# Converting the weights in units of 1024 columns, the low parts written over their own words

## The chip, the cores and the metric

The kernel runs on one core of a Trainium2 chip. The metric is the device time of one execution in microseconds (us). Before the change the median of three runs is 1238.58 us (1236.67 to 1239.37).

## The reference

An attention with random features comes first: 8 batches, 8 heads, 576 positions, 64 numbers each, 128 features. Its output, 4608 tokens of 512 numbers, goes through a gated layer.

```python
def phi(x):
    proj = np.einsum('bhsd,md->bhsm', x, omega)
    sq = np.sum(x * x, axis=-1, keepdims=True) / 2.0
    h = proj - sq
    h = h - np.max(h, axis=-1, keepdims=True)
    return np.exp(h) / np.sqrt(m)
...
kv = np.einsum('bhsm,bhsd->bhmd', k_p, v)
z = np.sum(k_p, axis=2)
num = np.einsum('bhsm,bhmd->bhsd', q_p, kv)
den = np.einsum('bhsm,bhm->bhs', q_p, z)[..., None] + 1e-06
...
gate = 1.0 / (1.0 + np.exp(-(x @ w_gate)))
val = x @ w_val
return (gate * val @ w_out).astype(np.float32)
```

The inputs of the attention are float32. The three weights, w_gate and w_val (512 x 1536) and w_out (1536 x 512), are float64. The kernel gets them as pairs of 32-bit words, a low and a high one, and turns them into float32 itself; this conversion is what is changed.

## The kernel before, in words

**Stages.** The program has four stages. In the first some 30 us only the attention of the first heads runs. Then, to about 510 us, the attention of all heads runs interleaved with a first pass of the gated layer: the tiles `gv` (L247), products of the tokens `xe` with the first 4 of 12 column tiles of the gate and value weights, `wh` and `wl`. From 600 us a second pass computes the other columns (`gw`, L351), and from about 965 us the output product follows (`po`, L465). The last two read weights that were converted during the attention and stored in DRAM as `w32`.

**Products in two parts.** A float32 matrix is split in a high part, rounded on ScalarE (ACT, L70), and a low part, the rest, subtracted on VectorE (DVE) or GpSimd (POOL) (L71); a product takes three matmuls. In the attention the inputs `rawk` and `rawq` are split into `hik`, `lok`, `hiq`, `loq`; `ppk` and `ppq` are their projections. DVE takes their maxima (`mxk`, `mxq`, L552), combines them with the norms (`hmk`, `hmq`, L556; `nb`, L574; `subq`, L613), forms `hq` (L615) for the queries, and ACT the exponentials `kpk` (L587) for the keys; `pkv`, `ptq`, `pnq`, `pxq` are the matmuls that follow, with `denq`, `invq`, `xq` on DVE (L643 to L649) between the last two.

**Conversion.** A unit is 1024 columns of weights. There are 18: the four units `e` (`first_weights`), whose result is split at once into `wh` and `wl` for the first pass, and 14 units `c` (`convert_weights`), to which four differences are added on POOL (L180) before they are stored as `w32` (L181). A unit lives in a tile `cv` of 7 x 512 words per partition, of which there are two in turn: 1024 results, 2048 words of raw pairs, and a scratch of 512. Two loads of 512 pairs each fill it (L144). Then `from_float64` runs for one half after the other: with the high word, five instructions on DVE make the float32 `t` of the high word (L78 clears the sign, L81 bounds it, L85 shifts it, L88 puts the sign back) and the power of two that belongs to it (L92, into the scratch `a`); L94 scales the low word by that power, in the scratch; and L96, on POOL, adds this to `t`. The second half's L78 writes the scratch that the first half's L96 reads.

**Order.** Python generators hand out the steps: one step of a conversion for every 32 steps of the attention (`EVERY`) at first, later one per step of the first pass. Each engine works through its own queue in order; the tile framework's scheduler places each instruction in that queue, as the lists below show, and inserts the waits on other engines. A DMA is issued by SP's queue, also in order.

Of the kernel before, what the change touches and what calls it, by code (L numbers as in the profile page):

```python
# [9 lines left out]
F32 = mybir.dt.float32  # L10
F32R = mybir.dt.float32r
AF = mybir.ActivationFunctionType
ALU = mybir.AluOpType
AX = mybir.AxisListType
U32 = mybir.dt.uint32
# [5 lines left out]
P = 128  # L21
# [10 lines left out]
LARGEST = float(np.uint32(0x47EFFE00).view(np.float32))  # L32
LEAST = float(np.uint32(0x38000000).view(np.float32))
# [8 lines left out]
WE = 2 * KC * P  # L42
WP = 512
# [24 lines left out]
def split(nc, hi, lo, x, lo_engine=None):  # L68

    nc.scalar.activation(out=hi, in_=x, func=AF.Copy)  # L70
    (lo_engine or nc.vector).tensor_tensor(out=lo, in0=x, in1=hi.bitcast(F32), op=ALU.subtract)  # L71


def from_float64(nc, t, a, bits):


    lo, hi = bits[:, :, 0], bits[:, :, 1]
    nc.vector.tensor_scalar(out=a, in0=hi, scalar1=0x7FFFFFFF, scalar2=None, op0=ALU.bitwise_and)  # L78

    f = a.bitcast(F32)  # L80
    nc.vector.tensor_scalar(  # L81
        out=f, in0=f, scalar1=LARGEST, scalar2=LEAST, op0=ALU.min, op1=ALU.max
    )

    nc.vector.tensor_scalar(  # L85
        out=t, in0=a, scalar1=3, scalar2=0x3FFFFFFF, op0=ALU.logical_shift_left, op1=ALU.bitwise_and
    )
    nc.vector.scalar_tensor_tensor(  # L88
        out=t, in0=hi, scalar=0xC0000000, in1=t, op0=ALU.bitwise_and, op1=ALU.bitwise_or
    )  # L90

    nc.vector.tensor_scalar(out=a, in0=t, scalar1=0xFF800000, scalar2=None, op0=ALU.bitwise_and)  # L92
    r = a.bitcast(F32)
    nc.vector.scalar_tensor_tensor(out=r, in0=lo, scalar=2.0**-52, in1=r, op0=ALU.mult, op1=ALU.mult)  # L94
    x = t.bitcast(F32)
    nc.gpsimd.tensor_tensor(out=x, in0=x, in1=r, op=ALU.add)  # L96


@with_exitstack
def attn_glu_kernel(ctx: ExitStack, tc, qT, kT, qn, kn, va, om, ident, w, out):  # L100
    nc = tc.nc
# [35 lines left out]

    def converted(cv, i):


        raw = [cv[:, (1 + h) * 2 * WP : (2 + h) * 2 * WP] for h in range(2)]
        for h in range(2):
            o = i + h * WP
            nc.sync.dma_start(out=raw[h].rearrange("p (n two) -> p n two", two=2), in_=w[:, o : o + WP, :])  # L144
        yield
        for h in range(2):
            from_float64(
                nc, cv[:, h * WP : (h + 1) * WP], cv[:, 6 * WP :],
                raw[h].rearrange("p (n two) -> p n two", two=2),
            )  # L150
            yield

    def first_weights(pool, tiles):

        for j in range(NE):
            cv = tiles(f"e{j}")
            ws[j] = wh, wl = [pool.tile([P, WE], F32R, name=f"{t}{j}") for t in ("wh", "wl")]
            steps = converted(cv, j * WE)
            next(steps)
            for i in range(2):  # L160
                next(steps)
                s = slice(i * WP, (i + 1) * WP)
                split(nc, wh[:, s], wl[:, s], cv[:, s].bitcast(F32), lo_engine=nc.gpsimd)
                yield

    def convert_weights(tiles, ns):

        for n in ns:
            cv = tiles(f"c{n}")
            for _ in converted(cv, NE * WE + n * 4 * Q):  # L170
                yield
            f = cv[:, : 4 * WP].bitcast(F32).rearrange("p (b q) -> p b q", q=Q)
            b, t = f[:, :4], f[:, 4:]
            for o, x, y in (
                (t[:, 0], b[:, 3], b[:, 0]),
                (t[:, 2], b[:, 2], b[:, 3]),
                (t[:, 1], b[:, 2], t[:, 0]),
                (t[:, 3], b[:, 1], t[:, 1]),
            ):
                nc.gpsimd.tensor_tensor(out=o, in0=x, in1=y, op=ALU.subtract)  # L180
            nc.sync.dma_start(out=w32[n], in_=f)  # L181
# [10 lines left out]
    def unit(pool, n, lo_engine=None):  # L192


        u = pool.tile([P, 2, N_OPS, Q], F32R, tag="u", bufs=UL if pool is late else UE, name=f"u{n}")
        units[n] = u[:, 0], u[:, 1]
        whole = u[:, 1].bitcast(F32)
        keep_order = pin if lo_engine else lambda x: x
        keep_order(nc.sync.dma_start(out=whole[:, :3], in_=w32[n, :, :3]))
        keep_order(nc.sync.dma_start(out=whole[:, 3:], in_=w32[n, :, 4:]))  # L200
        yield

        half = UL + UE <= n < UL + UE + EP
        for o, engine in ((slice(0, 3), nc.vector), (slice(3, N_OPS), lo_engine or nc.vector)):
            hi, lo, x = u[:, 0, o], u[:, 1, o], whole[:, o]
            if half:
                keep_order(nc.scalar.activation(out=hi, in_=x, func=AF.Copy, scale=0.5))
                keep_order(
                    nc.vector.scalar_tensor_tensor(
                        out=lo, in0=x, scalar=0.5, in1=hi.bitcast(F32), op0=ALU.mult, op1=ALU.subtract  # L210
                    )
                )
                continue
            keep_order(nc.scalar.activation(out=hi, in_=x, func=AF.Copy))
            keep_order(engine.tensor_tensor(out=lo, in0=x, in1=hi.bitcast(F32), op=ALU.subtract))
        yield
# [464 lines left out]
    def attention(pool):  # L681

        active = []
        while True:
            while True:
                kinds = [name[0][0] for name, _ in active]
                free = [
                    i for i, (name, needs, _) in enumerate(tasks[:AHEAD])
                    if (ready(Q) or name[1] == name[-1] == 0) and done.issuperset(needs) and kinds.count(name[0][0]) < ACTIVE[name[0][0]]
                ]  # L690
                if not free or len(active) >= AT_ONCE:
                    break
                name, _, make = tasks.pop(free[0])
                active.append((name, make(pool)))
            if not active:
                return
            name, steps = active.pop(0)
            if next(steps, steps) is steps:
                done.add(name)
            else:  # L700
                active.append((name, steps))
                yield

    def ready(n):

        return all(through[p] * P >= n for p in range(NP))
# [4 lines left out]
    with tc.tile_pool(name="early", bufs=1) as early:  # L711
        gates = first_pass()
        with tc.tile_pool(name="a", bufs=1, side="right") as pool:
            steps = attention(pool)

            def tiles(name):
                return pool.tile([P, 7 * WP], U32, tag="cv", bufs=2, name=name)

            conv = first_weights(early, tiles)
            cycle[:] = ["at", "at", "at", "gv"]  # L720
            n = 0
            while not ready(Q):
                next(steps, None)
                n += 1
                if n % EVERY == 0:
                    next(conv, None)
            cycle.clear()
            later = convert_weights(tiles, range(N_LATE))
            n = credit = 0
            while not ready(B * S):  # L730
                next(gates)
                credit += RATE if n >= 4 * NE - 2 else FIRST
                while credit >= 1 and not ready(B * S):
                    next(steps, None)
                    credit -= 1
                n += 1
                if next(conv, conv) is conv and n >= FROM:
                    next(later, None)
            for _ in later:
                pass  # L740
        late = ctx.enter_context(tc.tile_pool(name="late", bufs=1, side="right"))
        cycle[:] = ["at", "at", "at", "gv"]

        left = 2 * NE * (NCH + 1) - n
        started, parts = [], iter(())
        for n, _ in enumerate(gates):
            if n == 2:
                started = [unit(late, n) for n in range(UL)]
                for one in started:
                    next(one)  # L750
            elif started and n % 3 == 0:
                next(started.pop(0))
            if n == left - 2 * NE:
                parts = operands(0)
                x = next(parts)
            elif n > left - 2 * NE:
                next(parts, None)
        assert not started
# [107 lines left out]
```

## Time and profile before

| | |
|---|---|
| median of three runs | 1238.58 us |
| the profiled execution | 1239.43 us, of which its span is 1237.6 us |
| mean granted TensorE clock | 0.968 |
| ACT busy | 530.7 us (43%) |
| POOL busy | 542.7 us (44%) |
| share of the chain that ended last | PE 71%, DVE 12%, issue 7%, DMA 5%, POOL 3% |

PE is the matmul part of TensorE, PEld its weight load. The span runs from the first to the last instruction of the program; the execution's own time is 1.8 us longer. In a row of a group stand the line, the engine, the operation, the output and inputs by the program's names, the shapes, the count, then the busy time in us with the mean duration in ns, then the idle time of that engine just ahead of these instructions and what ended it. A line of a timeline has start and duration in us, then the same, with the idle time ahead of it and its releaser in square brackets.

### The profile page before, as it was taken

Reading aid. Unit: us, or ns where it says so; the run is one execution under the profiler, and the core shown is the slowest. Engines: PE = TensorE matmul, PEld = TensorE weight load, DVE = VectorE, ACT = ScalarE, POOL = GpSimd, SP = SyncE. Lnnn points to the kernel's source line nnn. Section 1 sums busy time; section 2 is a strip of 40 time slices with the busy share of each in tenths; the row PEclk is TensorE's granted clock in tenths of the full one; section 3 lists DMA queues with packets and bytes.
Section 4 is the critical chain, followed back from the end, with each engine's and each line's share of the span. In section 5 each row is a group of like instructions: output and inputs, shape, how many; then the busy total and the mean of one; then the engine's idle time right before and its main releaser. Section 6 shows DMA issues by size and latency. Waiting matters only on the chain.

```text
span 1237.6 us, 23990 instructions
## 1 busy us (share of the span) xinstructions
PE 1172.3 (95%) x8828; PEld 1109.8 (90%) x8828; DVE 864.5 (70%) x1907; ACT 530.7 (43%) x1164; POOL 542.7 (44%) x599
## 2 busy tenths in 40 slices
PE   6798989999898999899899999999998899999998
PEld 5788978798887888788899999999998899999998
DVE  4889888999698866433566656666569777777773
ACT  5556755565455463342423322232325344343331
POOL 2454365556457552131466666666666211111110
PEclk7798989999899999899899999999999999999999
DMA  7667767786657641461432333323337676666662
GB/s 247 213 199 228 210 219 253 238 268 237 226 182 252 223 153 39 139 202 52 152 128 106 123 135 124 121 93 125 124 135 267 203 226 195 188 191 189 198 191 94
DMA packets 104950, 219.43 MB, mean 177 GB/s; under 512 B 11136, under 2 KB 42112, under 8 KB 103040
## 3 DMA queue, kind: packets, MB, share of 16 engines
q1 hardware_dynamic: 87984, 198.94, 48.5%
q10 hardware_dynamic: 16848, 18.95, 4.4%
q8 instruction: 70, 1.15, 0.4%
q14 instruction: 48, 0.39, 0.1%
HBM read 141.82 MB, written 76.02 MB: 176 GB/s over the span
## 4 chain that ended last, share of the span: by engine, by line
PE 71%; DVE 12%; issue 7%; DMA 5%; POOL 3%; ACT 1%; SPq 1%; ACTq 0%; DVEq 0%; POOLq 0%
PE gw L351 27%; PE po L465 20%; PE gv L247 10%; PE pkv L595 4%; PE pnq L638 4%; PE ptq L626 2%; DVE mxq L552 2%; DVE hq L615 1%; DMA xr<-xT 1%; DMA xT<-xsq 1%; DMA rawk<-kT 1%; POOL loq L71 1%; DVE hmq L556 1%; PE ppk L547 1%; POOL xe L71 1%
## 5 line engine op out<-in xcount | busy, mean ns | idle before, releaser
L351 PE MATMUL gw<-xl,u 128*128 128x256 f32 x3024 | 364.6, 283 | 6.9 <-ACT p L362 3.6
L351 PEld LDWEIGHTS gw<-xl,u 128*128 128x128 f32 x3024 | 363.5, 191 | 7.9 <-DVE u L331 3.9
L465 PE MATMUL po<-u,yh 128*128 128x256 f32 x1512 | 272.4, 283 | 0.0
L465 PEld LDWEIGHTS po<-u,yh 128*128 128x128 f32 x1512 | 234.8, 191 | 0.0
L465 PE MATMUL po<-u,yl 128*128 128x256 f32 x756 | 214.0, 283 | 3.3 <-DVE yl L71 3.3
L247 PE MATMUL gv<-xe,wh 128*128 128x512 f32 (+1 forms) x640 | 201.0, 388 | 2.1 <-POOL xe L71 2.1
L70 ACT ACTIVATE yh<-yr 128x896 fp32r<-128x896 f32 x108 | 100.2, 950 | 156.8 <-PE po L465 86.3
L465 PEld LDWEIGHTS po<-u,yl 128*128 128x128 f32 x756 | 144.3, 191 | 3.9 <-DVE yl L71 3.9
L247 PEld LDWEIGHTS gv<-xe,wh 128*128 128x128 f32 x640 | 117.3, 194 | 20.1 <-POOL xe L71 4.5
L71 POOL TENSOR_TENSOR yl<-yr,yh 128x896 fp32r<-128x896 f32 x17 | 38.0, 2232 | 215.3 <-PE po L465 139.9
L247 PE MATMUL gv<-xe,wl 128*128 128x512 f32 (+1 forms) x320 | 125.8, 394 | 2.7 <-POOL wl L71 1.6
L71 DVE TENSOR_TENSOR yl<-yr,yh 128x896 fp32r<-128x896 f32 x91 | 103.0, 1144 | 31.5 <-PE po L465 19.1
L331 DVE TENSOR_TENSOR u<-gw,p 128x256 f32<-128x256 f32 x144 | 60.7, 422 | 59.2 <-PE gw L351 51.1
L595 PE MATMUL pkv<-v,kpk 128*128 128x66 f32 x512 | 84.4, 290 | 13.3 <-ACT kpk L587 12.6
L595 PEld LDWEIGHTS pkv<-v,kpk 128*128 128x128 f32 x512 | 77.0, 209 | 21.5 <-ACT kpk L587 19.8
L71 POOL TENSOR_TENSOR lok<-rawk,hik 128x256 fp32r<-128x256 f32 (+1 forms) x80 | 55.5, 712 | 68.0 <-ACT hik L70 67.6
L456 DVE TENSOR_TENSOR yr<-yr 128x128 f32<-128x128 f32 x144 | 60.1, 451 | 35.3 <-DMA yr<-ye 34.8
L71 POOL TENSOR_TENSOR xe<-xr,xe 128x512 fp32r<-128x512 f32 (+1 forms) x40 | 49.1, 1244 | 74.2 <-ACT xe L70 62.4
L71 POOL TENSOR_TENSOR loq<-rawq,hiq 128x256 fp32r<-128x256 f32 (+1 forms) x80 | 56.5, 718 | 55.5 <-ACT hiq L70 54.7
L587 ACT ACTIVATE kpk<-ppk,nb 128x128 f32<-128x128 f32 x256 | 69.8, 393 | 17.4 <-DVE nb L574 17.1
L638 PEld LDWEIGHTS pnq<-kv,qpq 128*128 128x128 f32 (+1 forms) x640 | 70.5, 189 | 6.5 <-ACT qpq L628 4.3
L638 PE MATMUL pnq<-kv,qpq 128*128 128x66 f32 (+1 forms) x640 | 74.9, 273 | 1.4 <-ACT qpq L628 1.2
(108 smaller groups left out, 2166.6 us busy)
## 6 DMA issues: line engine op xcount, KB each, us to landing
yl<-yl SPq DMA_DIRECT2D x36, 896.0 KB, 3.8
yr<-yl SPq DMA_DIRECT2D x72, 448.0 KB, 3.5
xr<-xT SPq DMA_DIRECT2D x68, 256.0 KB, 4.7
c<-w SPq DMA_DIRECT2D x28, 512.0 KB, 5.1
w<-c SPq DMA_DIRECT2D x14, 1024.0 KB, 4.5
v<-va SPq DMA_DIRECT2D x32, 330.0 KB, 3.4
natk<-kn SPq DMA_DIRECT2D x36, 256.0 KB, 4.2
natq<-qn SPq DMA_DIRECT2D x36, 256.0 KB, 3.9
```

The costliest lines, as they stand in the source:

```text
L70: nc.scalar.activation(out=hi, in_=x, func=AF.Copy)
L71: (lo_engine or nc.vector).tensor_tensor(out=lo, in0=x, in1=hi.bitcast(F32), op=ALU.subtract)
L247: nc.tensor.matmul(gv, lhsT=u[:, s], rhs=v, start=(m == 0), stop=(m == 3 * KC - 1))
L331: return nc.vector.tensor_tensor(out=o, in0=a, in1=b, op=ALU.add)
L351: nc.tensor.matmul(o, lhsT=u[:, k, s], rhs=v[:, kc, :], start=(first and m == 0), stop=(m == 5), skip_group_check=not first,)
L456: nc.vector.tensor_tensor(out=raw[:, o], in0=raw[:, a], in1=raw[:, b], op=op)
L465: nc.tensor.matmul(o, lhsT=u[:, i, :], rhs=v[:, k, :], start=(j + m == 0 and n in (1, 6, 5, 4)), stop=(j == NPAIR - 1 and m == 2), skip_gr ...
L552: nc.vector.tensor_reduce(out=m.rearrange("p t h -> p (t h)"), in_=pp, axis=AX.X, op=ALU.max)
L587: nc.scalar.activation(out=kp[t][:, h, :], in_=pp[:, 2 * i + h, :], func=AF.Exp, bias=nb[:, t - t0, h : h + 1], scale=SCALE,)
L595: nc.tensor.matmul(pkv[:, h, :], lhsT=kp[b * MID + i][:, h, :], rhs=v[:, i, h, :], start=(i == 0), stop=(i == MID),)
L626: nc.tensor.transpose(out=pt[:, i, :], in_=h_sb[:, i, :], identity=id_sb)
L638: nc.tensor.matmul(pn[r, 2 * i + h, :], lhsT=qp[:, 2 * i + h, r], rhs=kvs[u, p, bb][:, h, :], start=True, stop=True,)
```

## The change

`from_float64` now works on a whole unit, 1024 columns, in one go: six instructions on DVE and one on POOL per unit instead of twelve and two. There is no scratch: the first four steps run in place in the result tile, and the power of two (L93 in the new file) is written over the high words of the raw pairs, every second word, where L95 multiplies it with the low words in place; POOL's addition reads it from there. One load of 1024 pairs takes the place of two. The function is a generator that yields between the third and the fourth instruction, so that a unit still takes as many steps as before. The split of a unit `e` into `wh` and `wl` is done once for 1024 columns after the whole conversion, not after each half. The tile `cv` is 6 x 512 words.

```diff
-def from_float64(nc, t, a, bits):
+def from_float64(nc, t, bits):
     lo, hi = bits[:, :, 0], bits[:, :, 1]
-    nc.vector.tensor_scalar(out=a, in0=hi, scalar1=0x7FFFFFFF, scalar2=None, op0=ALU.bitwise_and)
-    f = a.bitcast(F32)
+    nc.vector.tensor_scalar(out=t, in0=hi, scalar1=0x7FFFFFFF, scalar2=None, op0=ALU.bitwise_and)
+    x = t.bitcast(F32)
     nc.vector.tensor_scalar(
-        out=f, in0=f, scalar1=LARGEST, scalar2=LEAST, op0=ALU.min, op1=ALU.max
+        out=x, in0=x, scalar1=LARGEST, scalar2=LEAST, op0=ALU.min, op1=ALU.max
     )
     nc.vector.tensor_scalar(
-        out=t, in0=a, scalar1=3, scalar2=0x3FFFFFFF, op0=ALU.logical_shift_left, op1=ALU.bitwise_and
+        out=t, in0=t, scalar1=3, scalar2=0x3FFFFFFF, op0=ALU.logical_shift_left, op1=ALU.bitwise_and
     )
+    yield
     nc.vector.scalar_tensor_tensor(
         out=t, in0=hi, scalar=0xC0000000, in1=t, op0=ALU.bitwise_and, op1=ALU.bitwise_or
     )
-    nc.vector.tensor_scalar(out=a, in0=t, scalar1=0xFF800000, scalar2=None, op0=ALU.bitwise_and)
-    r = a.bitcast(F32)
+    nc.vector.tensor_scalar(out=hi, in0=t, scalar1=0xFF800000, scalar2=None, op0=ALU.bitwise_and)
+    r = hi.bitcast(F32)
     nc.vector.scalar_tensor_tensor(out=r, in0=lo, scalar=2.0**-52, in1=r, op0=ALU.mult, op1=ALU.mult)
-    x = t.bitcast(F32)
     nc.gpsimd.tensor_tensor(out=x, in0=x, in1=r, op=ALU.add)
+    yield
...
     def converted(cv, i):
-        raw = [cv[:, (1 + h) * 2 * WP : (2 + h) * 2 * WP] for h in range(2)]
-        for h in range(2):
-            o = i + h * WP
-            nc.sync.dma_start(out=raw[h].rearrange("p (n two) -> p n two", two=2), in_=w[:, o : o + WP, :])
+        bits = cv[:, 2 * WP :].rearrange("p (n two) -> p n two", two=2)
+        nc.sync.dma_start(out=bits, in_=w[:, i : i + 2 * WP, :])
         yield
-        for h in range(2):
-            from_float64(
-                nc, cv[:, h * WP : (h + 1) * WP], cv[:, 6 * WP :],
-                raw[h].rearrange("p (n two) -> p n two", two=2),
-            )
-            yield
+        yield from from_float64(nc, cv[:, : 2 * WP], bits)
...
             next(steps)
-            for i in range(2):
-                next(steps)
-                s = slice(i * WP, (i + 1) * WP)
-                split(nc, wh[:, s], wl[:, s], cv[:, s].bitcast(F32), lo_engine=nc.gpsimd)
-                yield
+            next(steps)
+            yield
+            next(steps)
+            split(nc, wh, wl, cv[:, :WE].bitcast(F32), lo_engine=nc.gpsimd)
+            yield
...
-                return pool.tile([P, 7 * WP], U32, tag="cv", bufs=2, name=name)
+                return pool.tile([P, 6 * WP], U32, tag="cv", bufs=2, name=name)
```

The instructions also take other places in the queues. Three places follow. The new file is 7 lines shorter behind the conversion, so L587 of before is L580 there, L180 is L173, and so on.

On ACT, at about 33 to 40 us, before: `wh_289<-e_288` is the split of the first half of the first unit, `kpk_2_0` the first exponentials of the third head pair's keys.

```order
L70 ACTIVATE hiq_2_0_503<-rawq_2_0_477 128x256
L70 ACTIVATE hiq_3_0_513<-rawq_3_0_490 128x256
L70 ACTIVATE hiq_1_2_538<-rawq_1_0_265 128x256
L70 ACTIVATE wh_289<-e_288 128x512
L70 ACTIVATE hiq_0_2_557<-rawq_0_0_269 128x256
L501 ACTIVATE x2k_5_735<-natk_5_733 128x512
L587 ACTIVATE kpk_2_0_345<-ppk_2_0_318,nb_2_0_343 128x128 x4
```

The same place now:

```order
L70 ACTIVATE hiq_2_0_496<-rawq_2_0_470 128x256
L70 ACTIVATE hiq_3_0_506<-rawq_3_0_483 128x256
L70 ACTIVATE hiq_1_2_531<-rawq_1_0_265 128x256
L70 ACTIVATE hiq_0_2_550<-rawq_0_0_269 128x256
L580 ACTIVATE kpk_2_0_338<-ppk_2_0_311,nb_2_0_336 128x128 x4
L580 ACTIVATE kpk_2_2_343<-ppk_2_2_319,nb_2_0_336 128x128 x4
L580 ACTIVATE kmidk_2_4_348<-ppk_2_4_327,nb_2_0_336 128x128 x2
L580 ACTIVATE kpk_3_0_383<-ppk_3_0_356,nb_3_0_381 128x128 x4
L580 ACTIVATE kpk_3_2_388<-ppk_3_2_364,nb_3_0_381 128x128 x4
L580 ACTIVATE kmidk_3_4_393<-ppk_3_4_372,nb_3_0_381 128x128 x2
L593 ACTIVATE kv_2_0_411<-pkv_2_0_400 128x132
L70 ACTIVATE wh_289<-e_288 128x1024
```

The split stood four places ahead of the keys' exponentials; now it stands behind those of both head pairs and behind `kv_2_0`.

On POOL, at the first unit `c`, before (from about 133 us): L96 is the addition of a half, L180 the first of the four differences; the rows between are low parts for the attention.

```order
L96 TENSOR_TENSOR c_2882<-c_2882 128x512
L71 TENSOR_TENSOR lok_2_0_1873<-rawk_2_0_1810,hik_2_0_1872 128x256
L71 TENSOR_TENSOR lok_2_2_1877<-rawk_2_0_1810,hik_2_2_1876 128x256
L71 TENSOR_TENSOR lok_2_4_1881<-rawk_2_0_1810,hik_2_4_1880 128x128
L71 TENSOR_TENSOR loq_2_7_1920<-rawq_2_1_1268,hiq_2_7_1919 128x256
L71 TENSOR_TENSOR loq_3_7_1976<-rawq_3_1_1306,hiq_3_7_1975 128x256
L71 TENSOR_TENSOR lok_3_0_2064<-rawk_3_0_1990,hik_3_0_2063 128x256
L71 TENSOR_TENSOR lok_3_2_2068<-rawk_3_0_1990,hik_3_2_2067 128x256
L71 TENSOR_TENSOR lok_3_4_2072<-rawk_3_0_1990,hik_3_4_2071 128x128
L96 TENSOR_TENSOR c_2882<-c_2882 128x512
L180 TENSOR_TENSOR c_2882<-c_2882 128x256
```

The same unit now:

```order
L96 TENSOR_TENSOR c_2842<-c_2842 128x1024
L71 TENSOR_TENSOR lok_0_0_1479<-rawk_0_0_1233,hik_0_0_1478 128x256
L173 TENSOR_TENSOR c_2842<-c_2842 128x256 x4
L71 TENSOR_TENSOR lok_0_2_1483<-rawk_0_0_1233,hik_0_2_1482 128x256
L71 TENSOR_TENSOR lok_0_4_1487<-rawk_0_0_1233,hik_0_4_1486 128x128
```

One addition of 1024 stands where two of 512 stood nine places apart, and the unit comes earlier against the attention: ahead of `lok_0_0`, which before stood 15 places ahead of the unit's first addition.

On DVE, where the last unit `e` was converted, before (at about 104 to 108 us): L92 and L94 are that unit's second half; `denq` to `xq` are the divisions of two query tiles.

```order
L88 SCALAR_TENSOR_TENSOR e_1175<-e_1175 128x512
L503 TENSOR_REDUCE ssk_0_1263<-x2k_4_1456 128x8
L92 TENSOR_SCALAR e_1175<-e_1175 128x512
L643 TENSOR_SCALAR denq_1_4_1327<-pnq_1_4_1322 128x2
L94 SCALAR_TENSOR_TENSOR e_1175<-e_1175 128x512
L647 RECIPROCAL invq_1_4_1329<-denq_1_4_1327 128x2
L643 TENSOR_SCALAR denq_0_4_1342<-pnq_0_4_1337 128x2
L649 TENSOR_TENSOR xq_1_4_1331<-pnq_1_4_1322,invq_1_4_1329 128x128
```

The same divisions now:

```order
L608 SCALAR_TENSOR_TENSOR hq_0_4_1224<-ppq_0_4_1215,subq_0_4_1222 128x256
L496 TENSOR_REDUCE ssq_0_2101<-x2q_0_2104 128x8
L496 TENSOR_REDUCE ssq_0_2101<-x2q_1_2144 128x8
L636 TENSOR_SCALAR denq_1_4_1287<-pnq_1_4_1282 128x2
L78 TENSOR_SCALAR c_3132<-c_3132 128x1024
L640 RECIPROCAL invq_1_4_1289<-denq_1_4_1287 128x2
L636 TENSOR_SCALAR denq_0_4_1302<-pnq_0_4_1297 128x2
L642 TENSOR_TENSOR xq_1_4_1291<-pnq_1_4_1282,invq_1_4_1289 128x128
```

The unit `e` is done some 30 rows earlier there, and between `denq_1_4` and its reciprocal stands the first instruction of the second unit `c`, not the last of a unit `e`.

## The prediction

> **What bounds the kernel now.** I read the page's busy shares first, then the busy time by stage, then the conversion's own rows, then the chain of waits.
>
> ```profile
> PE 1172.3 (95%) x8828; PEld 1109.8 (90%) x8828; DVE 864.5 (70%) x1907; ACT 530.7 (43%) x1164; POOL 542.7 (44%) x599
> core 0: us, PE busy (x) PEld busy (x) DVE busy (x) ACT busy (x) POOL busy (x), PEclk, DMA share, GB/s
> 0.00:34.00 34.00, 21.86 (x106) 20.97 (x106) 15.90 (x34) 18.25 (x50) 10.20 (x20) 0.80 0.74 250
> 34.00:110.00 76.00, 63.38 (x441) 59.00 (x440) 64.31 (x159) 46.10 (x131) 38.92 (x42) 0.84 0.65 210
> 110.00:450.00 340.00, 320.02 (x2287) 286.80 (x2288) 292.53 (x745) 191.41 (x526) 183.16 (x215) 0.96 0.67 223
> 600.00:1237.00 637.00, 626.36 (x5217) 624.80 (x5216) 425.53 (x830) 215.88 (x336) 277.44 (x292) 1.00 0.47 155
> ```
>
> By the page the matmuls bound everything. The table by stage says where that is not all: from 600 us PE is busy 626 of 637 us at a clock of 1.00, and nothing of this change happens there. From 34 to 450 us PE is busy 383 of 416 us and runs at 0.84 and 0.96, while DVE is busy 357. Two engines near their limit hand work back and forth; a link on DVE shows as a gap on PE, and some gaps are followed by a lowered clock. Nearly all of the 18 conversions run there, the last addition of a `c` at 447.
>
> **The instructions themselves.** The rows of the tile `c` give minimum, median and maximum in ns; the three window rows are the busy time, up to 510 us, on DVE and POOL of tile `c`, on DVE, ACT and POOL of tile `e`, and on POOL of line 96.
>
> ```profile
> L78 DVE TENSOR_SCALAR c<-c x28: 409/424/1496, 102.4 to 434.1; 128x512 uint32<-128x512 uint32 x28
> L85 DVE TENSOR_SCALAR c<-c x28: 394/418/922, 114.8 to 440.5; 128x512 uint32<-128x512 uint32 x28
> L94 DVE SCALAR_TENSOR_TENSOR c<-c x28: 660/682/1350, 131.9 to 446.2; 128x512 f32<-128x512 uint32 x28
> L96 POOL TENSOR_TENSOR c<-c x28: 1269/1285/1662, 133.1 to 447.0; 128x512 f32<-128x512 f32 x28
> L180 POOL TENSOR_TENSOR c<-c x56: 722/740/1193, 154.3 to 450.5; 128x256 f32<-128x256 f32 x56
> 0.00:510.00 510.00, 99.64 (x168) 81.54 (x84) 0.94 0.62 207
> 0.00:510.00 510.00, 28.75 (x48) 5.29 (x8) 21.25 (x16) 0.94 0.62 207
> 0.00:510.00 510.00, 47.72 (x36) 0.94 0.62 207
> L615 DVE SCALAR_TENSOR_TENSOR hq<-ppq,subq 128x512 f32<-128x512 f32 x64 | 42.8, 679 | 0.1
> ```
>
> The last line is wanted for the slope and has its partner here:
>
> ```profile
> L615 DVE SCALAR_TENSOR_TENSOR hq<-ppq,subq 128x256 f32<-128x256 f32 x16 | 6.4, 412 | 0.0
> ```
>
> Per unit DVE now runs eight instructions with one input (0.42 us) and four with two (0.68): 6.1 us undisturbed, 18 x 6.1 = 109 of the 99.6 + 28.8 = 128.4 us that it is busy with them; the other 19 us are times when single ones took up to 1.5 us. For 1024 columns a two-input instruction goes from 0.412 over 0.679 by another 0.534 to 1.21 us. The one-input kind shows no second size: it lies between 0.42 (no growth) and 0.84 (double); I take 0.69, half of the other kind's slope, since 512 columns in 0.42 against 0.68 says that it moves them about twice as fast. A unit then costs 4 x 0.69 + 2 x 1.21 = 5.2 us, and 18 units save **16 us of DVE time** (36 down to 6 at the ends). POOL's addition grows by the slope from 0.740 to 1.285 to 2.37 us; 18 of them in place of 36 save 18 x (2.57 - 2.37) = **3.5 us of POOL time**.
>
> **Every second word.** L93 writes, L95 reads and writes, and POOL reads the high words at a step of two words. Reading so is in the trace: L78 reads the high words (0.424) where L85 reads a dense tile (0.418). Writing so is not, nor POOL reading so. From below I put nothing. From above: L93 takes 1.21 us instead of 0.69 (18 x 0.52 = 9 us of DVE), L95 and POOL's addition double (22 and 43 us). I take nothing, by L78, and keep the ends for the range.
>
> The Trainium skill's page "GPSIMD Engine Reference", section "Performance pitfalls for Q7 kernels", says that POOL pays half as much again per element when it reads with a step of more than 8 bytes. The step here is 8 bytes, so by the page it is free; were it over the limit, the 18 additions would take some 21 us longer, by the share below 4 us of the sum. No run here shows it yet.
>
> **What lies on the path.** In the chain that ended last, followed in order of time to 480 us, 52 pieces are DVE's conversion instructions, 7 are line 96, and 51 are the small DVE steps `hmq` and `subq`. First and last of each:
>
> ```profile
> 56.07 0.34 DVE e L78
> 440.54 0.34 DVE c L85
> 33.81 1.23 POOL e L96
> 415.51 1.24 POOL c L96
> 55.06 0.28 DVE hmq L556
> 469.45 0.68 DVE hmq L556 x2
> 0.00:510.00 510.00, 43.14 (x160) 0.94 0.62 207
> ```
>
> They sum to 30.8, 9.3 and 16.5 us; the window row is the busy time of `hmq` and `subq`. So 30.8 / 128.4 = 24% of the conversion's DVE time, 9.3 / 47.7 = 19% of POOL's additions and 16.5 / 43.1 = 38% of the small steps stand on the chain. Saved DVE time is worth 16 x 24% = **-3.9 us**, saved POOL time 3.5 x 19% = **-0.7**.
>
> **Waits removed.** The tile row names who held an instruction back (us, times):
>
> ```profile
>   POOL c L96: 6.9, 4
>   DMA c<-w: 2.6, 1
> L78 DVE TENSOR_SCALAR e<-e 128x512 uint32<-128x512 uint32 x8 | 4.5, 560 | 4.6 <-DMA e<-w 4.2 <-POOL e L96 0.5
> ```
>
> DVE stood 6.9 + 0.5 us at L78 until POOL had read the scratch. That goes: 7.4 x 24% = **-1.8**. What is late next is DVE's own queue, where 86% of the time from 34 to 450 us is work. The single load must land whole before L78 starts; of 36 halves two waited for a load (2.6 and 4.2 us), so its cover is the DVE work queued ahead. I put 0; if each of 18 units waited 2.6 us it would be 18 x 2.6 x 24% = +11. In SP's queue 18 issues fall away, which nobody waits for.
>
> **Longer holds.** This is what speaks against the change:
>
> ```profile
> 109.48 1.29 POOL L71 TENSOR_TENSOR wl<-e,wh 128x512 fp32r<-128x512 f32 x1 [0.74 <-ACT wh L70]
> 109.57 1.23 DVE L556 SCALAR_TENSOR_TENSOR hmq<-mxq,sqq 128x2 f32<-128x2 f32 x1
> ```
>
> An `hmq` of two columns took 1.23 us and ended 0.03 us after POOL's subtraction: small DVE steps with two inputs wait until POOL's instruction is over. One hold of 2.37 in place of two of 1.285 can cost 0 to 1.09 us more per unit, as DVE has work that is not held for less or more of it. I take a quarter, 0.27, since the medians above lie at the minima (most instructions are not held): 18 x 0.27 x 38% = **+1.9**; at the full 1.09, +7.5.
>
> The Trainium skill's "SBUF — State Buffer", section "Who interferes with whom", has the pair: a DVE instruction with two SBUF inputs contends with a POOL instruction that reads SBUF, and in DVE's two-port modes the loser waits for the whole instruction. The trace agrees (1.23 us here). Taken to the letter for every addition, the sum loses those 7.5 instead of 1.9.
>
> **Two gaps by name.**
>
> ```profile
> 35.06 0.63 ACT L70 ACTIVATE wh<-e 128x512 fp32r<-128x512 f32 x1 [1.22 <-POOL e L96]
> 36.82 1.36 PE L595 MATMUL pkv<-v,kpk 128*128 128x66 f32 x5 [2.80 <-ACT kpk L587]
> 106.25 1.15 DVE L94 SCALAR_TENSOR_TENSOR e<-e 128x512 f32<-128x512 uint32 x1
> 107.94 0.45 PE L655 MATMUL pxq<-id_sb,xq 128*128 128x128 f32 x1 [2.35 <-DVE invq L647]
> 110.83 0.58 PE L247 MATMUL gv<-xe,wl 128*128 128x256 f32 x1 [1.59 <-POOL wl L71]
> 105.00:114.00 9.00, 5.06 (x27) 4.51 (x25) 7.62 (x22) 3.82 (x10) 6.21 (x8) 0.62 0.59 157
> ```
>
> ACT stood 1.22 us ahead of `wh` with the keys' exponentials queued behind it, and PE waited 2.80 us for them; the order above puts `wh` behind them. At 110.83 PE waited 1.59 us for the last `wl`, which now comes earlier. Of the 4.4 us I book **-2.0**: 1.22 and half of 1.59, since 1.23 of POOL is in the share already.
>
> **The sum:** -3.9 - 0.7 - 1.8 + 1.9 - 2.0 = -6.5. A shortened link lets the next one end last, and PE, with 94% in 110 to 450 us, has little room; I keep 70%, -4.6. From the profiled execution's 1239.43 that is 1234.8; it stood 0.85 above the median of the runs, so **1234.0** in their terms.
>
> **Rivals.**
>
> Given back. PE's 94% decides, and the holds cost their full 7.5: -6.5 + 5.6 = -0.9, so 1237.7. For it: DVE's and POOL's queues are reordered everywhere, and the holds are seen. Against: half the additions, and the four L180 are untouched. 20%.
>
> Slower. A conversion instruction of 1.21 us, held by POOL for up to 2.37, stands ahead of one link of a division, as L94 stood ahead of `invq` at 106.25; PE then stops long enough to lose its clock. That place shows the price: a gap of 2.35, then 9 us at 0.62, which is 9 x 0.38 = 3.4 us; 5.8 together. One new place takes back the gain (-4.6 + 5.8 = +1.2), from the second on it is slower: +7.0, 1245.6. Against: there are 36 long two-input instructions now where there were 72 shorter ones. 20%.
>
> Better. The same price in the other direction: the places at 36 and 106 us keep their clock as well, -4.6 - 5.8 = -10.4, 1228.2. For it: the queue no longer has those rows ahead of the waiting ones. 15%.
>
> It doesn't do what it says. The step of two words costs L93 and L95 their upper ends: 31 us x 24% = +7.4 against -4.6, so 1241.4. Against: L78. 5%.
>
> **Numbers.** The forecast (1231 to 1236) has the other 40%. The range takes in the better case nearly whole, the slower one up to a single place with its holds: 1226 to 1244. Differences below 0.2% (2.5 us) count as none, about what a measurement of this kernel can tell. Faster: 40 + 15 = 55%. Same: 20% and a part of the others, 23%. Slower: 22%.
>
> **What would show it.** Two-input conversion rows at 1.21 us, one-input at 0.69 and line 96 at 2.37 with the minima near these; conversion on DVE at 105 to 115 us in place of 128; no wait of L78 on line 96; no PE gap by `kpk` at about 34 us; `hmq` and `subq` within 5 us of their 43. Fewer us at half clock before 510 us for the better case, more for the slower one. I am wrong if L93 or L95 lies above 1.3 us at its minimum, if L78 waits for loads in most units, or if the output product or the second pass changes by more than 2 us.

## The result, and the profile after

The forecast was 1234.0 us, faster. The changed kernel takes **1257.21 us** (median of 6 runs, 1250.85 to 1260.52) against 1237.62 before: a ratio of **1.0162, interval 1.0132 to 1.0191**, so slower by about 20 us. The profiled execution (1253.32 us, span 1251.5) is the second shortest of the six; it is 14 us longer than the profiled execution of before, where the medians differ by 20. One execution of the run with DVE's steps at the first halves' places, further down, was in a slower state of the chip and is left out of its median and ratio.

First the busy shares of the page after, then its busy time by stage; the columns are those of the prediction's table.

```profile
PE 1179.0 (94%) x8828; PEld 1115.9 (89%) x8828; DVE 857.7 (69%) x1799; ACT 531.4 (42%) x1160; POOL 543.9 (43%) x577
...
0.00:34.00 34.00, 21.57 (x106) 20.66 (x106) 15.90 (x35) 18.76 (x53) 11.14 (x21) 0.80 0.77 258
34.00:110.00 76.00, 66.47 (x367) 61.87 (x368) 58.03 (x117) 38.80 (x104) 33.26 (x29) 0.69 0.60 195
110.00:450.00 340.00, 307.65 (x2215) 275.18 (x2215) 283.79 (x644) 188.99 (x520) 186.88 (x199) 0.97 0.66 225
600.00:1237.00 637.00, 629.93 (x5228) 627.86 (x5227) 427.64 (x836) 222.99 (x347) 276.57 (x292) 0.99 0.48 161
```

From 34 to 110 us PE finished 367 matmuls where it had finished 441, at a clock of 0.69 where it had 0.84. Cut at 200 us, the same view of before and then of after says where the loss ends:

```profile
34.00:200.00 166.00, 147.44 (x1071) 138.18 (x1071) 142.02 (x364) 102.07 (x280) 81.66 (x93) 0.89 0.68 221
200.00:600.00 400.00, 376.66 (x2439) 325.84 (x2438) 281.04 (x682) 194.48 (x499) 173.40 (x195) 0.97 0.56 189
```

```profile
34.00:200.00 166.00, 140.50 (x920) 130.22 (x920) 132.68 (x292) 92.73 (x251) 78.69 (x79) 0.81 0.64 210
200.00:600.00 400.00, 377.36 (x2496) 327.81 (x2497) 278.84 (x632) 196.55 (x511) 177.49 (x187) 0.99 0.54 183
```

By 200 us 151 matmuls are missing. At 166 / 1071 = 0.155 us each, the mean before, that is an estimate of 23 us. From 200 to 600 us there are 57 more than before, which at 400 / 2439 = 0.164 us wins back 9. The 14 us that are left are the difference of the two profiled spans (1251.5 against 1237.6). PE idled 25.5 us in place of 18.6 from 34 to 200 us, and the lower clock (0.81 for 0.89 over 166 us) is up to 13 more.

The conversion's own rows, of the tile `c` after, and the busy time of the tiles `c` and `e` up to 510 us, of `hmq` (with `subq`) up to 530, where its last step lies now, and of line 96 up to 510, are as the prediction drew them:

```profile
L78 DVE TENSOR_SCALAR c<-c x14: 672/722/2376, 103.5 to 391.0; 128x1024 uint32<-128x1024 uint32 x14
L85 DVE TENSOR_SCALAR c<-c x14: 657/684/1674, 110.1 to 393.5; 128x1024 uint32<-128x1024 uint32 x14
L89 DVE SCALAR_TENSOR_TENSOR c<-c x14: 1194/1216/2321, 111.5 to 395.3; 128x1024 uint32<-128x1024 uint32 x14
L93 DVE TENSOR_SCALAR c<-c x14: 665/688/1657, 114.0 to 397.6; 128x1024 uint32<-128x1024 uint32 x14
L95 DVE SCALAR_TENSOR_TENSOR c<-c x14: 1194/1218/1226, 115.2 to 403.0; 128x1024 f32<-128x1024 uint32 x14
L96 POOL TENSOR_TENSOR c<-c x14: 2396/2420/2914, 119.1 to 404.3; 128x1024 f32<-128x1024 f32 x14
0.00:510.00 510.00, 83.18 (x84) 80.68 (x70) 0.92 0.61 204
0.00:510.00 510.00, 21.96 (x24) 4.22 (x4) 19.42 (x8) 0.92 0.61 204
0.00:530.00 530.00, 47.99 (x160) 0.92 0.59 199
0.00:510.00 510.00, 44.29 (x18) 0.92 0.61 204
```

DVE spends 83.18 + 21.96 = 105.1 us on the conversion, 23.3 less than before, and POOL 44.3 on the additions, 3.4 less. Writing at a step of two words costs nothing: L93 takes 0.688 us and L95 1.218, where L85 and L89, which write a dense tile, take 0.684 and 1.216. The time that was to be saved was saved, and the kernel is slower.

One of the new gaps, in the chain of waits of the changed kernel (start, us, what), in order of time:

```profile
119.11 2.37 POOL c L96
121.48 1.16 POOL lok L71
122.63 2.11 POOL c L173 x3
124.74 0.07 issue
124.81 0.73 POOL c L173
125.55 1.13 POOL lok L71 x2
126.67 0.02 issue
126.69 0.65 SPq L512
127.34 0.05 issue
127.39 6.17 DMA natk<-kn
```

```profile
134.60 0.39 PE L240 MATMUL gv<-xe,wl 128*128 128x256 f32 x1 [2.75 <-ACT ge L261]
```

POOL does the first unit `c` between two keys' low parts. SP's queue stands first at that unit's store, L174, for 4.2 us until the last of the four differences L173 is done, and then at the load L512, which waits for a `lok`. The load of `natk` behind them comes late, ACT waits for it with `ge` behind, and PE waits 2.75 us (the second fence, from PE's timeline). Before, the first store of a `c` was issued at 158 us, here at 125.6. This is one gap and an example; it does not show where the 23 us come from.

### The profile page after: what moved, and what is told of

The parts are those of the page before. It is cut to its first block, busy times and chain, and to the rows that moved or that the text cites. A ratio compares the mean times of both kernels' runs of the same rounds, so it can differ in the third digit from the quotient of the medians.

```text
span 1251.5 us, 23829 instructions
## 1 busy us (share of the span) xinstructions
PE 1179.0 (94%) x8828; PEld 1115.9 (89%) x8828; DVE 857.7 (69%) x1799; ACT 531.4 (42%) x1160; POOL 543.9 (43%) x577
## 4 chain that ended last, share of the span: by engine, by line
PE 74%; DVE 11%; DMA 6%; issue 4%; POOL 3%; ACT 2%; SPq 1%; ACTq 0%; DVEq 0%; POOLq 0%
PE gw L344 27%; PE po L458 20%; PE gv L240 11%; PE pnq L631 4%; PE pkv L588 4%; PE ptq L619 2%; DMA natk<-kn 1%; DVE mxq L545 1%; DMA xT<-xsq 1%; PE ppk L540 1%; DVE hmq L549 1%; PE pxq L648 1%; PE ppk L541 1%; POOL xe L71 1%; PE ppk L542 1%
## 5 line engine op out<-in xcount | busy, mean ns | idle before, releaser
L71 POOL TENSOR_TENSOR loq<-rawq,hiq 128x256 fp32r<-128x256 f32 (+1 forms) x80 | 59.9, 761 | 78.1 <-ACT hiq L70 78.0
L71 POOL TENSOR_TENSOR xe<-xr,xe 128x512 fp32r<-128x512 f32 (+1 forms) x40 | 49.9, 1264 | 87.3 <-ACT xe L70 85.9
L580 ACT ACTIVATE kpk<-ppk,nb 128x128 f32<-128x128 f32 x256 | 69.6, 391 | 15.3 <-DVE nb L567 15.2
```

The source lines that it names most:

```text
L580: nc.scalar.activation(out=kp[t][:, h, :], in_=pp[:, 2 * i + h, :], func=AF.Exp, bias=nb[:, t - t0, h : h + 1], scale=SCALE,)
```

## The experiments

### One part undone

In these kernels the scheduler makes its own order anew. Ratios are to the kernel before, on the same chip, with 95% intervals. The texts of what was expected name theories of the loss: load (one transfer of 1 MB in place of two), length (long single instructions), place (where the scheduler puts the conversion), and later split, unit and order.

**Two loads again:**

```diff
-        nc.sync.dma_start(out=bits, in_=w[:, i : i + 2 * WP, :])
+        for h in range(2):
+            s = slice(h * WP, (h + 1) * WP)
+            nc.sync.dma_start(out=bits[:, s, :], in_=w[:, i + h * WP : i + (h + 1) * WP, :])
```

> The changed kernel with each unit loaded in two DMAs of 512 pairs again; the order of the DVE conversion steps among the attention's steps stays that of the changed kernel (the first nine units the same, counted by hq). Load theory (one transfer of 1 MB delays the natk and raw loads behind it in SP's queue): 1238 to 1246 us. Length theory (DVE steps of 1.22 us and POOL additions of 2.42 us stand ahead of small links) and place theory (the scheduler puts the conversions earlier, into the stretch from 34 to 200 us where DVE has no room): both 1252 to 1262.

Measured 1249.93, **1.0089** (1.0060 to 1.0119): between the theories.

**The addition in halves** (`for s in halves: nc.gpsimd.tensor_tensor(out=x[:, s], ...)`):

> The changed kernel with POOL's addition in two instructions of 512 columns; DVE's order unchanged. Length theory, as far as POOL's instructions hold DVE's small steps: 1240 to 1248, and hmq and subq fall towards the 43 us of before. If it is DVE's own length, or the place, or the load: 1252 to 1262.

Measured 1259.51, **1.0160** (1.0106 to 1.0214). The time did not move, but `hmq` and `subq` did not get shorter either: they take 49.9 us in this run's trace, against 48.0 in the changed kernel. So this run alone does not acquit POOL's holds.

**All steps in pieces** (the same loop around each of the six DVE steps too):

> The changed kernel with each of the six DVE steps and the addition issued as two instructions of 512 columns, in the same steps of the generator, one load. With these the scheduler goes back to an order close to that of before (the last unit ends at the 62nd hq, 55th in the changed kernel, 68th before). Length and place theories: 1234 to 1242. Load theory: 1250 to 1260.

Measured 1263.09, **1.0202** (1.0172 to 1.0232). In its trace `hmq` and `subq` take 44.7 us, near the 43.1 of before, and the time is no better: the loss is there without the longer holds. Short instructions alone don't help either, as far as a run can say in which the scheduler's order moved too.

**The kernel before, only without its scratch:**

```diff
-def from_float64(nc, t, a, bits):
+def from_float64(nc, t, bits):
...
-                nc, cv[:, h * WP : (h + 1) * WP], cv[:, 6 * WP :],
+                nc, cv[:, h * WP : (h + 1) * WP],
```

> The kernel before, half by half with two loads, but with the low parts written over their words and no scratch, so that only the wait of L78 for POOL's addition goes. Length, place and load theories: 1232 to 1240, the forecast's own booking of that wait was -1.8 us. If writing over the words costs by itself: above 1245.

Measured **1225.99** (1224.30 to 1233.52), **0.9898** (0.9872 to 0.9924): better than both kernels. It is called the version by halves below.

### One part added to the version by halves

**One load for a whole unit:**

> The version in place by halves (1226 us) with one load of 1024 pairs for a unit. Load theory (the first half can only start when 1 MB has landed, and natk and the raws queue behind it): 1232 to 1242, some 7 us as between the changed kernel and the one with two loads. Split theory and unit theory: 1223 to 1231.

Measured 1241.28, **1.0025** (0.9994 to 1.0055).

**One split for a whole unit `e`:**

```diff
-            for i in range(2):
-                next(steps)
-                s = slice(i * WP, (i + 1) * WP)
-                split(nc, wh[:, s], wl[:, s], cv[:, s].bitcast(F32), lo_engine=nc.gpsimd)
-                yield
+            next(steps)
+            yield
+            next(steps)
+            split(nc, wh, wl, cv[:, :WE].bitcast(F32), lo_engine=nc.gpsimd)
+            yield
```

> The version in place by halves with the split of a unit e into wh and wl done once for 1024 columns behind both halves, as the changed kernel does. Split theory (the early stage to 110 us loses because ACT's 1.06 us and POOL's 2.36 us instructions stand ahead of exponentials and low parts): 1234 to 1246. Load theory and unit theory (what costs is that a unit goes through the six steps as one piece, so that POOL's addition comes only behind all of DVE's work): 1223 to 1231.

Measured 1249.42, **1.0094** (1.0057 to 1.0130).

The next is the version in pieces with two loads and with the splits looped over halves; the last is the changed kernel with those two.

> Steps of 512 columns, two loads, splits of 512 columns, in place; only the order differs from the version by halves: each step for both halves before the next step, a pause behind the third. Unit theory: 1245 to 1262, near the one with pieces (1263). Load theory: 1250 to 1257. Split theory, or load and split together: 1224 to 1236.

Measured 1255.35, **1.0131** (1.0071 to 1.0192).

> The changed kernel with two loads and with the splits of e in halves of 512: DVE's six instructions of 1024 and POOL's one stay. Split theory: 1228 to 1240. Unit theory and length: 1246 to 1256, as with two loads alone (1250).

Measured 1262.39, **1.0191** (1.0146 to 1.0236), though two loads alone had 1.0089.

These results don't add up: each single part costs 15 to 29 us against 1226, and undoing two parts is worse than undoing one. The scheduler can answer every edit with another order of all instructions. The table counts, in one trace of each kernel, the conversion's DVE steps that start ahead of the 24th `hq`, and gives the time at which that `hq` starts:

| kernel | conversion steps done by then | 24th `hq` at, us | median, us |
|---|---|---|---|
| before | 68 of 216 | 178.6 | 1238 |
| before, in place | 70 of 216 | 181.9 | 1226 |
| halves, one load | 71 of 216 | 176.2 | 1241 |
| halves in pieces, half splits | 73 of 216 | 181.2 | 1255 |
| halves, one split | 75 of 216 | 188.1 | 1249 |
| changed, in pieces | 77 of 216 | 191.8 | 1263 |
| changed, two loads, half splits | 43 of 108 | 187.6 | 1262 |
| changed, two loads | 45 of 108 | 195.3 | 1250 |
| changed, addition in halves | 45 of 108 | 201.9 | 1260 |
| changed | 45 of 108 | 198.7 | 1257 |

The changed kernel has done 42% of its conversion where the kernel before had done 31%, about 1.8 units more. But the column does not put the kernels in the order of their times: 45 of 108 go with 1250 us and 73 of 216 with 1255.

### The order held fixed

To part the order from the instructions, the next kernels carry a table of places for every engine, turned into edges that only order. In their traces PE, DVE, ACT and POOL run all instructions other than the conversion's in exactly the order meant, by the program's names:

```diff
+def in_order(tc, nc):
...
+            if before is not None:
+                tc.add_manual_dep(
+                    own[at], before.name,
+                    mybir.DependencyInfo(mybir.DependencyClass.NoSync, mybir.DependencyReason.DATA),
+                    reason="in_order",
+                )
+            before = own[at]
```

> The version in place by halves (1226 us by the scheduler's own order) in exactly the order of the kernel before: only the scratch and with it the wait of L78 are gone. If that wait is what made it faster: 1226 to 1232; by the forecast's booking of -1.8 and the order theory: 1234 to 1239.

Measured 1238.26, **1.0005** (0.9979 to 1.0030). No gain is seen from the scratch and its wait, though the interval still has room for the 1.8 us that were booked. The 12 us that the same instructions gain in the scheduler's own order come from that order.

> The other way round: the version in place by halves (instructions of 512 columns, two loads, split in halves), with all other instructions in exactly the order of the changed kernel; the two halves of a step stand side by side at the place of the whole step. Order theory: 1248 to 1264. Unit theory as far as the length goes: 1226 to 1240.

Measured 1263.89, **1.0230** (1.0186 to 1.0274).

> All other instructions in exactly the order of the changed kernel, as in the run of the halves in the new order (1264), but DVE's halves are spread: the second half's step at the place of the whole step, the first half's a few instructions ahead of it, so that other work stands between them. If the changed kernel's order itself costs the time: 1250 to 1266. If only the dense placing of a unit's steps does: 1232 to 1244.

Measured 1263.65, **1.0210** (1.0187 to 1.0233). In the spread version 45 conversion steps of 216 stand right behind another one on DVE, as against 44 in the kernel before and 117 side by side. The same halves of 512 columns, spread or side by side, lose 25 us in the changed kernel's order. The window of 34 to 200 us follows, first of the halves in the old order, then of the two in the new one. The profiled executions of these two are the longest of their runs (1276.5 and 1269.7 us):

```profile
34.00:200.00 166.00, 147.16 (x1065) 137.22 (x1064) 142.23 (x355) 101.16 (x275) 81.42 (x93) 0.89 0.68 219
```

```profile
34.00:200.00 166.00, 140.86 (x910) 131.50 (x910) 134.22 (x327) 92.08 (x253) 81.26 (x90) 0.79 0.63 206
```

```profile
34.00:200.00 166.00, 137.95 (x920) 127.42 (x920) 134.29 (x334) 93.72 (x255) 81.04 (x90) 0.84 0.64 208
```

They finish 910 and 920 matmuls in place of 1065; the changed kernel finished 920. **The new order, with the conversion at its new places, gives the changed kernel's loss in the same stage without any long instruction.** `hmq` and `subq` take 41.9 us in the first of the two, so longer holds have no part in it. From 200 to 600 us the two win nothing back: they finish 2421 and 2439 matmuls, where the halves in the old order finish 2460 and the changed kernel 2496.

Whole units in the old orders:

> The changed kernel's own instructions (six DVE steps and one addition of 1024 columns, one load, one split, in place), but every other instruction on every engine in exactly the order of the kernel before, fixed by edges that only order; a unit e takes the places of its first half, a unit c those of its second half. Order theory (the time is lost because the scheduler answers the changed conversion with another order of the attention's instructions): 1226 to 1240, the forecast's sum being -4.6. Unit theory (whole units and long instructions cost by themselves): 1248 to 1262.

Measured 1266.89, **1.0237** (1.0205 to 1.0270).

> The same instructions in the order of the version in place by halves (1226 us). Order theory: 1218 to 1234. Unit theory: 1245 to 1262.

Measured 1245.06, **1.0082** (1.0052 to 1.0113), against 0.9898 for the halves in that order. So the order is not all: whole units lose 19 to 29 us in orders that suit halves, and both theories, each taken as the only one, fall. The windows of 34 to 200 and 200 to 600 us of the whole units in the order of before:

```profile
34.00:200.00 166.00, 141.20 (x992) 132.41 (x991) 132.70 (x294) 93.27 (x255) 73.45 (x77) 0.86 0.61 198
200.00:600.00 400.00, 373.66 (x2422) 324.00 (x2421) 272.58 (x632) 194.15 (x509) 174.90 (x191) 0.97 0.55 189
```

Against the halves at the same order, 1065 and 2460, both stages are behind. Each such row is of one execution, and the medians decide on the times.

### What a whole unit costs at a fixed order

> The version in place by halves in the order of before (1238), with one load of 1 MB at the place of the first of its two; all else as it was. Load theory (a half waits for the whole megabyte, and others share the transfer): 1245 to 1260. Length theory and place theory: 1235 to 1241.

Measured 1237.64, **1.0009** (0.9983 to 1.0035): no cost of the single load is seen.

> In the order of before, with instructions of 512 columns and two loads, but both halves of a step side by side, at the places at which the whole steps stood in the run with whole units in the old order (1267). Place theory (a unit's work comes at half as many places, twice as dense): 1255 to 1270. Length theory: 1238 to 1248; the same for the load theory.

Measured 1258.42, **1.0178** (1.0142 to 1.0215): the dense placing of a unit's steps is the greater part.

> Whole units in the order of before (1267) with two loads of 512 pairs at their old places instead of one. Load theory: 1240 to 1254. Length and place theories: 1258 to 1272.

Measured 1262.95, **1.0215** (1.0185 to 1.0246): the length and the single split of a unit `e` add some 5 us together, and the intervals overlap.

> In the order of before, two loads; only the fourteen units c are whole (instructions of 1024 columns at the places of their second halves), the four units e go by halves at their old places. If the loss sits in the first weights, behind which the exponentials of the keys wait: 1236 to 1245. If it sits in the units c: 1252 to 1268.

Measured 1252.11, **1.0113** (1.0077 to 1.0148): the units `c` alone cost 14 us, somewhat more than half of the 25. That the first weights make the rest is the difference; it was not tried by itself.

The windows of 34 to 200 and 200 to 600 us with the halves side by side (the halves at their own places had 1065 in the first and 2460 in the second):

```profile
34.00:200.00 166.00, 146.44 (x1084) 136.25 (x1083) 143.15 (x356) 102.26 (x281) 81.29 (x94) 0.90 0.68 220
200.00:600.00 400.00, 370.51 (x2372) 320.73 (x2371) 272.11 (x677) 187.81 (x493) 173.02 (x196) 0.97 0.53 180
```

Short steps side by side lose nothing by 200 us and 88 matmuls behind it, another stage than the new order. With whole units `c` alone it is the same stage: 1071 and 2421. The largest gap there in the run with whole units `c`, whose profiled execution (1244.18 us) is the shortest of its run, has this chain of waits:

```profile
209.93 0.08 POOL c L245
210.01 0.08 issue
210.09 0.02 POOLq L71
210.10 0.51 issue
210.62 0.75 POOL lok L71
211.36 0.02 issue
211.38 0.33 SPq L584
211.71 0.05 issue
211.76 4.11 DMA xr<-xT
215.87 0.02 issue
215.90 0.63 ACT xe L70
216.53 0.26 ACT kpk L652
216.79 0.04 issue
216.83 0.67 PE pkv L660 x2
```

Again `lok` stands on POOL behind a unit's differences, SP's queue behind `lok`, a load behind that, and ACT's exponentials behind the load: PE was idle for 3.93 us. But the halves in the old order, which lose nothing, have the same chain at nearly the same times: `lok` at 210.01 us (here 210.62) and `xe` at 215.64 (here 215.90), with a PE gap of 0.57. Here the attention had come some 3 us further by then (one `hik` at 205.48 us, there at 208.45), and the gap takes that lead back. So the chain paces both kernels and does not tell them apart. Whether the addition's waiting on POOL makes the loss was tried last:

> As the run with only the units c whole in the order of before (1252), but DVE's whole steps stand at the places of the first halves; POOL's addition and all behind it stay where they were, so that the addition no longer stands in POOL's queue waiting for six long steps (38.7 us in 8 waits there). Queue theory (lok, loq and xe stand in POOL's queue behind an addition that waits for a whole unit's steps): 1236 to 1245. Density theory on DVE (the long steps themselves delay the links): 1248 to 1260.

Measured 1257.04, **1.0182** (1.0144 to 1.0221). The time lies where DVE's density was expected to put it, but the run does not decide. The addition's waits did go, and DVE's first step now stands in its own queue waiting for the load (of the tile `c`, what its engine waited for, then who waited for `c`):

```profile
  DMA c<-w: 14.7, 5
  DVE c L78: 16.1, 6
```

One wait took the place of another. Whether DVE's or POOL's queue makes the loss of a dense unit stays open.

## Why the prediction was wrong, point by point

- **The instructions: right.** The two-input steps took 1.218 us where 1.21 was forecast, the one-input steps 0.688 for 0.69, and the addition 2.420 for 2.37. DVE's conversion took 105.1 us, in the band of 105 to 115. L78 never waited for line 96; its one wait on POOL, of 4.1 us, was for a difference L173. POOL saved 3.4 us for the forecast 3.5. The step of two words was rightly put at nothing: the addition's 2.42 us compare with 2.36 for POOL's dense `wl` of the same size. The Trainium skill's "GPSIMD Engine Reference", section "Performance pitfalls for Q7 kernels", charges half as much again only for a step of more than 8 bytes; the trace agrees at 8 bytes, by these two times.
- **"Saved DVE time is worth 16 x 24%" = -3.9: the step that failed.** It priced the conversion by its share of a chain that belongs to the old order, with the work spread as before, and the sum had no term for the new order and the denser placing; they were put at nothing without a reason. DVE saved 23 us, more than the 16, and the kernel lost 20. Measured by themselves, the new order costs halves 25 us, and whole units cost 25 to 29 us in the old order. A share of the chain says what a conversion step costs where it stands, not what it costs where it will stand.
- **The scratch's wait, -1.8: not seen.** The in-place halves in the order of before gave 1.0005 (0.9979 to 1.0030), too wide to tell 1.8 us from nothing.
- **The load, booked at 0: right at a fixed order** (1.0009). In the changed kernel's own order two loads were 7 us better, but there the scheduler was free to move other things as well.
- **Longer holds, +1.9: the size came out, the reason is not borne out.** `hmq` and `subq` rose from 43.1 to 48.0 us, within the 5 us named, and 4.9 x 38% is the 1.9 that was booked. But they take 49.9 us with the addition cut in two, so the length of one addition does not explain the rise. The Trainium skill's "SBUF — State Buffer", section "Who interferes with whom", taken to the letter for every addition, would have put 7.5 on the sum, a rise of 18 x 1.09 = 19.6 us in these steps; the trace shows a quarter of that.
- **Two gaps, -2.0: both went.** The one at 34 us fell from 2.80 to 0.82, and from 95 to 134 us PE has no gap over 1 us, where it had 2.35 and 1.59. But the clock at 38 to 68 us was worse (below), and the gap of 2.75 us at 134.6 is new.
- **"Nothing of this change happens" from 600 us: nearly.** The second pass (`gw`) began 17.9 us later and ended 13.5 later, so it took 368.4 us in place of 372.8; the output product took 278.6 in place of 278.3. The change of 4.4 us is more than the 2 us that were named as a sign of being wrong.
- **The rivals.** The slower one had the kind of loss right (late links, PE gaps, lost clock) and was priced for two places, 1245.6. It was the whole stage from 34 to 200 us, 23 us. "DVE's and POOL's queues are reordered everywhere" stood under the rival of 1237.7 as if that could only cancel a gain.

What the runs show in its place is two effects that don't add. The order that the scheduler makes for whole units, the conversion's places included, costs halves some 25 us; whole units in the old order cost as much; both together, the changed kernel, cost 20. Why the new order is bad was not tried by itself. The table suggests that the conversion runs ahead: 1.8 units, at 105.1 / 18 = 5.8 us of DVE each, are 10.5 us more DVE work ahead of the same `hq`, in a stretch where DVE was busy 142 of 166 us already; and behind it, with PE busy 377 of 400 us, only 9 of the 23 us were won back. It is an argument from these rows, not shown, and one row speaks against it: whole units in the order of before reach the 24th `hq` as late as 190.8 us with only 32 of 108 steps done, so that `hq` can be late without the conversion running ahead.

## What to carry to other kernels

Where a scheduler places the instructions, the price of an edit is not the difference of its durations: run the old instructions in the new order and the new ones in the old order before believing either. A background job can cost more when it gets cheaper but denser: in the old order, steps of one length cost 20 us when they stood side by side and nothing when they stood apart. Standing apart is not enough, as the spread halves in the new order show. And a change may hold a part worth keeping: the same writing in place, by halves, ran at 0.9898 of the kernel before, by an order that suited it.

## What was not expected of the hardware

The granted TensorE clock did not follow the largest gap of PE. Before, the gap of 2.80 us from 34 us on was the largest up to 68 us; in the changed kernel it was 0.82 us, and up to 68 us none exceeded 1.18 (PE's timeline of the changed kernel, the first gap and the largest):

```profile
34.09 1.99 PE L588 MATMUL pkv<-v,kpk 128*128 128x66 f32 x8 [0.82 <-ACT kpk L580]
...
61.36 3.68 PE L631 MATMUL pnq<-kv,qpq 128*128 128x66 f32 x16 [1.18 <-ACT qpq L621]
```

Yet the window of 38 to 68 us, of before and then of after, reads:

```profile
38.00:68.00 30.00, 26.36 (x153) 24.54 (x154) 22.69 (x59) 14.94 (x40) 11.78 (x13) 0.72 0.56 182
```

```profile
38.00:68.00 30.00, 25.53 (x116) 23.44 (x116) 22.98 (x46) 13.21 (x29) 14.92 (x11) 0.50 0.64 210
```

PE was busy 25.5 of 30 us and held at a clock of 0.50 all the time, and it finished 116 matmuls in place of 153. The halves in the new order show the same 0.50, busy 25.80 us. What keeps the clock down is not shown. It is not the busy share alone: the halves side by side in the old order were busy 25.06 us at a clock of 0.72. Nor does the order settle it: the halves in the order of before had 0.61 at 26.45 us busy, where the kernel before had 0.72 at 26.36.
